# Agent attention and gated FFN: attention arithmetic moved to VectorE, POOL kept for transfers

## The chip, the cores and the metric

The kernel runs on one core of one Trainium2 chip. The metric is the device time of one launch in microseconds (us), lower is better. The times shown are the median of several runs, with the lowest and the highest.

## The reference

Four batches of 12480 tokens with 128 channels, and 49 agents per batch. `agent_v` is the attention of the agents over keys and values; each query then attends to the agents; the result goes through a feed-forward net with 2048 hidden units.

```
def sm(a, b):
    s = scale * (a @ b.transpose(0, 2, 1))
    s = s - s.max(-1, keepdims=True)
    e = np.exp(s)
    return e / (e.sum(-1, keepdims=True) + 1e-09)
agent_v = sm(agents, k) @ v
x = sm(q, agents) @ agent_v          # 4 x 12480 x 128
h = x @ w_in                         # 128 -> 2048
g = h * (1.0 / (1.0 + np.exp(-1.702 * h)))
out = g @ w_out                      # 2048 -> 128
```

All inputs are f32 (the weights arrive as 64-bit floats and are converted on the chip). Queries, keys and agents are scaled by 8, so the softmax is steep and the scores must be exact.

## The kernel before, in words

**Tiling.** A group is 960 tokens (`GT`, two halves of `CH` = 480). A batch has 13 groups (`NG`), and the hidden layer 16 slices of 128 (`NF`). One *step* is one slice of one group, so a batch has 208 steps and the kernel 832. In a step TensorE does `up` (L393: four products of 480 columns into two PSUM banks `ph`, of the pair `sa`, `sb` with the high and the low part of the folded weights `wh`, `wl`), ScalarE the gelu into `g`, and, five steps later (`LAG`), TensorE does `down` (L421: six products of 480 columns into `po`). To keep f32 accuracy with float32r products, `g` is split into a rounded part `gh` (L406) and the rest `gl` = `g` - `gh` (L416, always on VectorE). The rounding is done by a DMA issued from POOL's queue for the slices in `HI_ON_DMA`, by ScalarE for those in `HI_ON_ACT`, and by VectorE otherwise. For a slice rounded by DMA the `gl` subtraction is put two steps later (L671). `g` and `gl` have five tiles each, `gh` six.

**Attention.** It is woven into the steps. `agent_v` of the next batch is folded with `w_in` into `wh`, `wl` (L317, L331), so the feed-forward net takes softmax weights of 49 agents as its input. For that the next batch's 13 key blocks of 960 are loaded, split into three bf16 parts (`split`, L166: four pieces of 484 elements, POOL), multiplied with the agents (`scores`, L180: 32 products into two banks of `ps_m`, each reduced by VectorE at L197), the maximum taken (L240 to L261), and then, per block, shifted (L274, POOL), exponentiated (ScalarE), split into a high and a low part `e_pair` (L282: ScalarE, then POOL) and multiplied with the value block `v_pair`, also split (L288, L291, VectorE); the sums are added up in `acc` (L310). The queries of the next group go through the same `split` and `scores`, a softmax (L352 to L374) and four transposes (`query_pairs`, L377).

**Order.** From step 16 on, the order on TensorE, ScalarE, VectorE and POOL is the order of the program text (`manual_schedule`, L684); each engine's queue is worked off in that order. `put(t, fn)` hangs a job on step t. Within a step come `up`, the jobs, the rounding and `gl`, then `down` of the slice five steps back. `pe_step` (L587) moves a TensorE job to the next step that has none; steps 4 (`Q_AT`) and 13 (`P_AT`) of each group are reserved for query scores and transposes. Key blocks follow at five-step intervals from step 4 of the batch (from step 16 in the first), value blocks at steps 3 and 12 of the groups after that. So a batch has a stage with key blocks, about its first four groups, and a stage with the maximum, the value blocks and the weights; the last batch has neither.

**Buffers around the change.** `ps_m` has two banks for scores, transposes, value sums and weights. `rest` (the parts of a split) and the working tiles have two tiles, the loads `kt`, `vt` together three, `qt` two. `e_pair` and `v_pair` are single. SP issues the loads and the stores.

Of the kernel before, what the change touches and what calls it, by code (L numbers as in the profile page):

```python
# [40 lines left out]
def kernel(  # L41
# [44 lines left out]
    e_pair = const.tile([P, KB, P], F32R, name="e_pair")  # L86
    nc.gpsimd.memset(e_pair.bitcast(F32), 0.0)
# [78 lines left out]
    def split(t):  # L166
        r = work.tile([P, GT + PAD], F32, name="rest", tag="rest")
        nc.gpsimd.memset(t[:, GT:], 0.0)
        n = (GT + PAD) // 2

        def piece(i):
            s = slice(i % 2 * n, (i % 2 + 1) * n)
            if i < 2:
                nc.gpsimd.tensor_sub(out=r[:, s], in0=t[:, s], in1=halves(t)[0][:, s])  # L174
            else:
                nc.gpsimd.tensor_sub(out=halves(r)[1][:, s], in0=r[:, s], in1=halves(r)[0][:, s])  # L176

        return (halves(t)[0], halves(r)[0], halves(r)[1]), piece

    def scores(b, parts, out):  # L180
        x0, x1, x2 = parts
        a = ag_part[:, b].rearrange("p i a -> p (i a)")
        mm = nc.tensor.matmul
        for c in range(2):
            ps = ps_m.tile([P, 512], F32, name="ps_m")
            for j in range(KB // 2):
                t0 = (c * KB // 2 + j) * TB
                t = slice(t0, t0 + P)
                o = ps[:, j * 2 * A : (j + 1) * 2 * A]
                mm(out=o, lhsT=x0[:, t], rhs=a[:, 0 : 2 * A], start=True, stop=False)  # L190
                mm(out=o[:, A:], lhsT=x0[:, t], rhs=a[:, 2 * A :], start=False, stop=False)
                mm(out=o, lhsT=x1[:, t], rhs=a[:, 0 : 2 * A], start=False, stop=False)  # L192
                mm(out=o[:, 0:A], lhsT=x2[:, t], rhs=a[:, 0:A], start=False, stop=True)
            s = ps[:TB, : KB * A].rearrange("p (j i a) -> p j i a", i=2, a=A)
            o = out[:, c * KB // 2 : (c + 1) * KB // 2, :]
            if RED:
                nc.vector.tensor_reduce(out=o, in_=s.rearrange("p j i a -> p j a i"), axis=AX.X, op=ALU.add)  # L197
            else:
                nc.scalar.copy(out=o, in_=s[:, :, 0, :])
                nc.vector.tensor_add(out=o, in0=s[:, :, 1, :], in1=o)  # L200
# [94 lines left out]
    def key_matmuls(g, ps, first, last):  # L295
        for j in range(KB):
            nc.tensor.matmul(  # L297
                out=ps[:, : 2 * C + 2],
                lhsT=e_pair[:TB, j, :],
# [17 lines left out]
    def weights_sums(acc, w):  # L317
        ps = ps_m.tile([P, 512], F32, name="ps_m")
        zc = work.tile([P, P], F32, name="zc", bufs=1)
        nc.vector.tensor_copy(out=zc, in_=acc[:, 2 * C : 2 * C + 1].broadcast_to([P, P]))  # L320
        nc.tensor.matmul(out=ps[:, 0:P], lhsT=acc[:, 0:C], rhs=sel, start=True, stop=False)
        nc.tensor.matmul(out=ps[:, 0:P], lhsT=acc[:, C : 2 * C], rhs=sel, start=False, stop=True)
        nc.tensor.matmul(out=ps[:, P : 2 * P], lhsT=zc, rhs=sel, start=True, stop=True)
# [23 lines left out]
    def query_scores(n, b, parts):  # L347
        sd = e_sb[n % 2][:TB, :, 0:A]
        scores(b, parts, sd)
# [66 lines left out]
    def low(g, gh):  # L416
        gl = gpool.tile([P, 2, CH], F32R, name="gl", bufs=LAG)
# [62 lines left out]
    def do_key_scores(b, g):  # L480
        key_scores(b, g, k_parts.pop((b, g)))
# [99 lines left out]
    pe_steps = {n * NF + f for n in range(B * NG) for f in (Q_AT, P_AT)}  # L581
# [16 lines left out]
    for b in range(B - 1):  # L598
        s0 = b * per_batch
        for k in range(NKG):  # L600
            t = pe_step(s0 + (NF if b == 0 else K_AT) + 5 * k)
            put(t - 13 if b else max(t - 13, 0), lambda b=b, k=k: do_key_load(b + 1, k))
            for i in range(4):
                put(max(t - 5 + i, s0), lambda b=b, k=k, i=i: do_key_split(b + 1, k, i))
# [121 lines left out]
```

## Time and profile before

| | |
|---|---|
| time, median of 3 runs | 2235.41 us (2225.12 to 2239.26) |
| profiled execution | 2236.78 us, span 2235.0 us |
| TensorE (PE) busy | 2108.1 us, 94% of the span |
| VectorE (DVE) busy | 1771.2 us, 79% |
| ScalarE (ACT) busy | 1579.3 us, 71% |
| GpSimd (POOL) busy | 737.7 us, 33% |
| mean granted TensorE clock | 0.979 |
| start of the first step, end of the last group | 73 us, 2224.2 us |

A row of the groups reads: line, engine, operation, output<-inputs with their shapes, count, then busy us and the mean ns of one, then the engine's idle time just before them and what ended most of it. A row of the waits reads: who waited, for whom, us in total, how often, the longest. A row of the stages reads: the stretch, its length, and the busy us of each engine with its instruction count, then granted clock, share of the DMA engines and GB/s. A row of the timeline reads: start, us, engine, line, operation, and in brackets the idle time before it and its releaser.

### The profile page before, as it was taken

What the parts mean: (1) busy time and instruction counts of PE and PEld (TensorE: products, weight loads), DVE (VectorE), ACT (ScalarE), POOL (GpSimd) and SP (SyncE); (2) the same over time, 40 slices, a digit from 0 to 9 for tenths busy, and PEclk for the clock granted to TensorE, in tenths of its full rate; (3) what the DMA queues carried; (4) which work ended last, traced back from release to release, by engine and by line L of the source; (5) the groups of instructions that cost most, each with busy time, mean ns of one, the idle gap of its engine ahead of it and who ended that gap; (6) DMA issues with size and microseconds to landing.
All of it is one profiled execution on the core that took longest, in us unless ns stands there. A gap on an engine that the chain in (4) does not pass through costs nothing.

```text
span 2235.0 us, 32467 instructions
## 1 busy us (share of the span) xinstructions
PE 2108.1 (94%) x12232; PEld 1794.0 (80%) x12232; DVE 1771.2 (79%) x1882; ACT 1579.3 (71%) x2563; POOL 737.7 (33%) x773
## 2 busy tenths in 40 slices
PE   8899998999999999999999999989999999999999
PEld 7688877888777788778778788778877888888887
DVE  6988888778778888888877887887886768776765
ACT  3566776677676678677667667767776887778886
POOL 3355624222135544322214664222221313121310
PEclk9999999999999999999999999999999999999999
DMA  9423412232223232232223233223222221212221
GB/s 263 142 89 107 133 63 80 92 112 80 80 96 99 89 103 93 80 106 98 81 79 106 89 114 108 66 90 114 85 71 71 71 98 63 98 63 87 73 80 62
DMA packets 79297, 210.87 MB, mean 94 GB/s; under 512 B 7580, under 2 KB 33500, under 8 KB 79140
## 3 DMA queue, kind: packets, MB, share of 16 engines
q1 hardware_dynamic: 49188, 106.55, 16.2%
q0 software_dynamic: 29952, 102.25, 13.0%
q8 instruction: 96, 1.57, 0.3%
q14 instruction: 61, 0.50, 0.1%
HBM read 80.97 MB, written 25.56 MB: 48 GB/s over the span
## 4 chain that ended last, share of the span: by engine, by line
PE 69%; DVE 18%; issue 8%; DMA 3%; ACT 1%; POOL 1%; DVEq 0%; ACTq 0%; SPq 0%; POOLq 0%
PE po L429 38%; PE ph L398 12%; PE ph L400 12%; DVE gl L418 11%; DMA gh<-g 2%; DVE gh L413 2%; PE ps_m L190 1%; PE ps_m L213 1%; PE ps_m L192 1%; DVE sb L389 1%; ACT g L403 1%; DVE sa L388 1%; PE ps_m L381 1%; PE ps_m L297 1%; DVE acc L314 1%
## 5 line engine op out<-in xcount | busy, mean ns | idle before, releaser
L418 DVE TENSOR_TENSOR gl<-g,gh 128x960 fp32r<-128x960 f32 x832 | 1131.7, 1385 | 393.1 <-DMA gh<-g 181.7
L403 ACT ACTIVATE g<-ph 128x480 f32<-128x480 f32 x1664 | 857.0, 573 | 424.3 <-PE ph L400 376.1
L429 PE MATMUL po<-gh,wo_h 128*128 128x480 f32 x1664 | 525.8, 397 | 0.2 <-ACT gh L411 0.2
L429 PE MATMUL po<-gl,wo_h 128*128 128x480 f32 x1664 | 503.7, 384 | 11.1 <-DVE gl L418 11.1
L429 PE MATMUL po<-gh,wo_l 128*128 128x480 f32 x1664 | 506.7, 386 | 0.0
L409 POOL DMA_DIRECT2D gh<-g x208 | 115.1, 553 | 1074.7 <-DVE gl L418 714.3
L411 ACT CAST gh<-g 128x960 fp32r<-128x960 f32 x416 | 415.1, 998 | 12.2
L429 PEld LDWEIGHTS po<-gl,wo_h 128*128 128x128 f32 x1664 | 317.2, 191 | 62.8 <-DVE gl L418 12.8
L429 PEld LDWEIGHTS po<-gh,wo_l 128*128 128x128 f32 x1664 | 317.3, 191 | 50.6
L429 PEld LDWEIGHTS po<-gh,wo_h 128*128 128x128 f32 x1664 | 303.2, 191 | 52.6 <-ACT o L440 8.4
L398 PE MATMUL ph<-sb,wh 128*128 128x480 f32 x832 | 320.7, 385 | 0.6 <-DVE sb L389 0.4
L398 PE MATMUL ph<-sa,wh 128*128 128x480 f32 x832 | 320.3, 385 | 0.7 <-ACT g L403 0.7
L400 PE MATMUL ph<-sa,wl 128*128 128x480 f32 x832 | 318.8, 383 | 0.0
L400 PE MATMUL ph<-sb,wl 128*128 128x480 f32 x832 | 316.8, 381 | 0.0
L176 POOL TENSOR_TENSOR rest<-rest 128x484 bf16<-128x484 f32 x182 | 271.1, 1507 | 0.4
L398 PEld LDWEIGHTS ph<-sb,wh 128*128 128x128 f32 x832 | 158.5, 190 | 34.4 <-ACT g L403 5.3
L398 PEld LDWEIGHTS ph<-sa,wh 128*128 128x128 f32 x832 | 159.3, 191 | 30.3 <-ACT g L403 1.4
L400 PEld LDWEIGHTS ph<-sb,wl 128*128 128x128 f32 x832 | 157.4, 189 | 25.7 <-issue 0.2
L400 PEld LDWEIGHTS ph<-sa,wl 128*128 128x128 f32 x832 | 157.7, 190 | 24.9 <-issue 0.2
L413 DVE CAST gh<-g 128x960 fp32r<-128x960 f32 x208 | 164.6, 792 | 2.1 <-ACT g L403 0.3
L174 POOL TENSOR_TENSOR rest<-qt 128x484 f32<-128x484 f32 x104 | 135.8, 1323 | 76.0 <-issue 21.7
L440 ACT COPY o<-po 128x480 f32<-128x480 f32 x104 | 53.2, 564 | 138.2 <-PE po L429 138.2
(103 smaller groups left out, 2055.9 us busy)
## 6 DMA issues: line engine op xcount, KB each, us to landing
gh<-g POOLq DMA_DIRECT2D x208, 480.0 KB, 2.9
kt<-kT SPq DMA_DIRECT2D x52, 480.0 KB, 3.6
qt<-qT SPq DMA_DIRECT2D x52, 480.0 KB, 3.4
vt<-v SPq DMA_DIRECT2D x52, 480.0 KB, 4.2
outT<-o SPq DMA_DIRECT2D x104, 240.0 KB, 2.6
words<-w_in SPq DMA_DIRECT2D x4, 512.0 KB, 11.9
words<-w_out SPq DMA_DIRECT2D x4, 512.0 KB, 8.6
ag_sb<-agT SPq DMA_DIRECT2D x1, 98.0 KB, 2.0
```

The source lines that it names most:

```text
L174: nc.gpsimd.tensor_sub(out=r[:, s], in0=t[:, s], in1=halves(t)[0][:, s])
L176: nc.gpsimd.tensor_sub(out=halves(r)[1][:, s], in0=r[:, s], in1=halves(r)[0][:, s])
L190: mm(out=o, lhsT=x0[:, t], rhs=a[:, 0 : 2 * A], start=True, stop=False)
L398: nc.tensor.matmul(out=ph[c][:, :CH], lhsT=wh[:, s], rhs=pairs[c], start=True, stop=False)
L400: nc.tensor.matmul(out=ph[c][:, :CH], lhsT=wl[:, s], rhs=pairs[c], start=False, stop=True)
L403: nc.scalar.activation(out=g[:, c, :], in_=ph[c][:, :CH], func=AF.Gelu_apprx_sigmoid)
L409: nc.gpsimd.dma_start(out=gh, in_=g)
L411: nc.scalar.copy(out=gh, in_=g)
L413: nc.vector.tensor_copy(out=gh, in_=g)
L418: nc.vector.tensor_sub(out=gl, in0=g, in1=gh.bitcast(F32))
L429: nc.tensor.matmul(out=po[c][:, :CH], lhsT=lhsT[:, f, :], rhs=rhs[:, c, :], start=(f == 0 and first), stop=(f == NF - 1 and last),)
L440: nc.scalar.copy(out=o, in_=po[c][:, :CH])
```

## The change

POOL's arithmetic inside the steps goes to VectorE: the four pieces of each split, now cut so that the first two belong to the first half of the tokens, the key shifts, and the low half of `e_pair`; the high half of `e_pair` goes there from ScalarE. (In the start, ahead of the steps, twelve shifts stay on POOL.) Six slices of 16 instead of four are rounded by DMA, two instead of four by VectorE, eight by ScalarE as before, and the `gl` of a DMA slice is put three steps after its product instead of two. Scores are computed in two pieces of one bank in two steps: steps 4 and 5 for queries, t and the next free step for keys; `e_pair` is doubled, `gl` has four tiles instead of five. Query exponentials move from step 7 to 8, sums and softmax with them, splits from 14 to 15; value blocks from steps 3 and 12 to 1 and 11; the first batch's key blocks start at step 10 instead of 16. The next weights are spaced: the copy `zc` two steps after the last value product, its products two or more after that, the first weight part three or more later. The diff, without the places that only carry the new argument through:

```diff
-E_AT = 7
+E_AT = 8
 P_AT = 13
-S_AT = 14
+S_AT = 15
 K_AT = 4
-V_AT = 3
-V2_AT = 12
+V_AT = 1
+V2_AT = 11
...
-HI_ON_DMA = (7, 8, 9, 11)
-HI_ON_ACT = (0, 2, 5, 6, 10, 12, 14, 15)
+HI_ON_DMA = (1, 3, 5, 10, 11, 14)
+HI_ON_ACT = (0, 2, 4, 6, 7, 12, 13, 15)
...
     def split(t):
         r = work.tile([P, GT + PAD], F32, name="rest", tag="rest")
         nc.gpsimd.memset(t[:, GT:], 0.0)
-        n = (GT + PAD) // 2
         def piece(i):
-            s = slice(i % 2 * n, (i % 2 + 1) * n)
-            if i < 2:
-                nc.gpsimd.tensor_sub(out=r[:, s], in0=t[:, s], in1=halves(t)[0][:, s])
+            s = slice(0, CH + PAD) if i < 2 else slice(CH + PAD, GT + PAD)
+            if i % 2 == 0:
+                nc.vector.tensor_sub(out=r[:, s], in0=t[:, s], in1=halves(t)[0][:, s])
             else:
-                nc.gpsimd.tensor_sub(out=halves(r)[1][:, s], in0=r[:, s], in1=halves(r)[0][:, s])
+                nc.vector.tensor_sub(out=halves(r)[1][:, s], in0=r[:, s], in1=halves(r)[0][:, s])
...
-    def scores(b, parts, out):
+    def scores(b, parts, out, c):
...
-        for c in range(2):
-            ps = ps_m.tile([P, 512], F32, name="ps_m")
+        ps = ps_m.tile([P, 512], F32, name="ps_m")
...
     def key_pair(g):
         sc = score[:TB, g * KB : (g + 1) * KB, :]
-        ep = e_pair
-        nc.scalar.copy(out=ep[:TB, :, 0:A], in_=sc)
-        nc.gpsimd.tensor_sub(out=ep[:TB, :, H : H + A], in0=sc, in1=ep[:TB, :, 0:A].bitcast(F32))
+        ep = e_pair[g % 2]
+        nc.vector.tensor_copy(out=ep[:TB, :, 0:A], in_=sc)
+        nc.vector.tensor_sub(out=ep[:TB, :, H : H + A], in0=sc, in1=ep[:TB, :, 0:A].bitcast(F32))
...
-        gl = gpool.tile([P, 2, CH], F32R, name="gl", bufs=LAG)
+        gl = gpool.tile([P, 2, CH], F32R, name="gl", bufs=LAG - 1)
...
-    pe_steps = {n * NF + f for n in range(B * NG) for f in (Q_AT, P_AT)}
+    pe_steps = {n * NF + f for n in range(B * NG) for f in (Q_AT, Q_AT + 1, P_AT)}
...
-            t = pe_step(s0 + (NF if b == 0 else K_AT) + 5 * k)
+            t = pe_step(s0 + (10 if b == 0 else K_AT) + 5 * k)
+            t1 = pe_step(t + 1)
...
-            put(t, lambda b=b, k=k: do_key_scores(b + 1, k))
-            put(t + 1, lambda k=k: key_part_max(k))
+            put(t, lambda b=b, k=k: do_key_scores(b + 1, k, 0))
+            put(t1, lambda b=b, k=k: do_key_scores(b + 1, k, 1))
+            put(t1 + 1, lambda k=k: key_part_max(k))
...
-            put(min(shift + 3 * k, slot - 1), lambda k=k: key_shift(k, nc.gpsimd.tensor_tensor))
+            put(min(shift + 3 * k, slot - 1), lambda k=k: key_shift(k, nc.vector.tensor_tensor))
             put(t - 16, lambda b=b, k=k: do_value_load(b + 1, k))
-            put(t - 3, lambda k=k: key_pair(k))
-            put(t - 4, lambda b=b, k=k: value_hi(k, vts[b + 1, k]))
-            put(t - 4, lambda b=b, k=k: value_lo(k, vts.pop((b + 1, k))))
+            put(t - 3, lambda b=b, k=k: value_hi(k, vts[b + 1, k]))
+            put(t - 3, lambda b=b, k=k: value_lo(k, vts.pop((b + 1, k))))
+            put(slot + 1, lambda k=k: key_pair(k))
...
-        put(pe_step(last + 2), lambda b=b, w=w: weights_sums(accs.pop(b + 1), w))
-        t = last + 3
+        put(t + 2, lambda b=b, w=w: weights_0(accs.pop(b + 1), w))
+        t = pe_step(t + 4)
+        put(t, lambda w=w: weights_1(w))
+        t = t + 2
...
-        put(s0 + Q_AT, lambda n=n: do_query_scores(n + 1))
-        put(s0 + Q_AT + 1, lambda n=n: do_query_load(n + 2))
-        put(s0 + Q_AT + 1, lambda n=n: do_query_shift(n + 1))
+        for c in range(2):
+            put(s0 + Q_AT + c, lambda n=n, c=c: do_query_scores(n + 1, c))
+        put(s0 + Q_AT + 2, lambda n=n: do_query_load(n + 2))
+        put(s0 + Q_AT + 2, lambda n=n: do_query_shift(n + 1))
...
-                at.setdefault(t + 2, []).insert(0, lambda t=t: live.update({t: (gh, low(g, gh))}))
+                at.setdefault(t + 3, []).insert(0, lambda t=t: live.update({t: (gh, low(g, gh))}))
```

`weights_0` holds the copy `zc` and `weights_1` the rest of the former `weights_sums`.

More of the change, by code (lines that the diff above doesn't have):

```diff
@@ L84 @@
         )
-    e_pair = const.tile([P, KB, P], F32R, name="e_pair")
-    nc.gpsimd.memset(e_pair.bitcast(F32), 0.0)
+    e_pair = []
+    for i in range(2):
+        t = const.tile([P, KB, P], F32R, name=f"e_pair{i}")
+        nc.gpsimd.memset(t.bitcast(F32), 0.0)
+        e_pair.append(t)
     v_pair = const.tile([P, KB, 2 * C + 2], F32R, name="v_pair")
@@ L183, in scores @@
         mm = nc.tensor.matmul
-        for c in range(2):
-            ps = ps_m.tile([P, 512], F32, name="ps_m")
[L186 to L200, printed above, removed]
+        ps = ps_m.tile([P, 512], F32, name="ps_m")
+        for j in range(KB // 2):
+            t0 = (c * KB // 2 + j) * TB
+            t = slice(t0, t0 + P)
+            o = ps[:, j * 2 * A : (j + 1) * 2 * A]
+            mm(out=o, lhsT=x0[:, t], rhs=a[:, 0 : 2 * A], start=True, stop=False)
+            mm(out=o[:, A:], lhsT=x0[:, t], rhs=a[:, 2 * A :], start=False, stop=False)
+            mm(out=o, lhsT=x1[:, t], rhs=a[:, 0 : 2 * A], start=False, stop=False)
+            mm(out=o[:, 0:A], lhsT=x2[:, t], rhs=a[:, 0:A], start=False, stop=True)
+        s = ps[:TB, : KB * A].rearrange("p (j i a) -> p j a i", i=2, a=A)
+        o = out[:, c * KB // 2 : (c + 1) * KB // 2, :]
+        nc.vector.tensor_reduce(out=o, in_=s, axis=AX.X, op=ALU.add)
     def key_load(b, g):
@@ L228, in first_key_scores, with key_scores @@
         )
-    def key_scores(b, g, parts):
-        s = score[:TB, g * KB : (g + 1) * KB, :]
-        scores(b, parts, s)
+    def key_scores(b, g, parts, c):
+        scores(b, parts, score[:TB, g * KB : (g + 1) * KB, :], c)
     def key_part_max(g):
@@ L298, in key_matmuls @@
                 out=ps[:, : 2 * C + 2],
-                lhsT=e_pair[:TB, j, :],
+                lhsT=e_pair[g % 2][:TB, j, :],
                 rhs=v_pair[:TB, j, :],
@@ L314, in key_sum, with weights_0, weights_1 @@
             nc.vector.tensor_add(out=acc, in0=ps[:, : 2 * C + 1], in1=acc)
-    def weights_sums(acc, w):
-        ps = ps_m.tile([P, 512], F32, name="ps_m")
+    def weights_0(acc, w):
         zc = work.tile([P, P], F32, name="zc", bufs=1)
         nc.vector.tensor_copy(out=zc, in_=acc[:, 2 * C : 2 * C + 1].broadcast_to([P, P]))
-        nc.tensor.matmul(out=ps[:, 0:P], lhsT=acc[:, 0:C], rhs=sel, start=True, stop=False)
-        nc.tensor.matmul(out=ps[:, 0:P], lhsT=acc[:, C : 2 * C], rhs=sel, start=False, stop=True)
-        nc.tensor.matmul(out=ps[:, P : 2 * P], lhsT=zc, rhs=sel, start=True, stop=True)
+        w["acc"], w["zc"] = acc, zc
+    def weights_1(w):
+        ps = ps_m.tile([P, 512], F32, name="ps_m")
+        nc.tensor.matmul(out=ps[:, 0:P], lhsT=w["acc"][:, 0:C], rhs=sel, start=True, stop=False)
+        nc.tensor.matmul(out=ps[:, 0:P], lhsT=w["acc"][:, C : 2 * C], rhs=sel, start=False, stop=True)
+        nc.tensor.matmul(out=ps[:, P : 2 * P], lhsT=w["zc"], rhs=sel, start=True, stop=True)
         rz = work.tile([P, P], F32, name="rz", bufs=1)
@@ L345, in query_load, with query_scores @@
         return t
[L347 removed]
+    def query_scores(n, b, parts, c):
         sd = e_sb[n % 2][:TB, :, 0:A]
[L349 removed]
+        scores(b, parts, sd, c)
         return sd
```

28 lines of the change are left out of this document (14 added, 14 removed).

## The prediction

> **What bounds the kernel now.** I read the page first, then the engines' busy time by stage, the list of waits, and the timeline of one group where a wait ends.
>
> ```profile
> PE 2108.1 (94%) x12232; PEld 1794.0 (80%) x12232; DVE 1771.2 (79%) x1882; ACT 1579.3 (71%) x2563; POOL 737.7 (33%) x773
> ```
>
> TensorE is the long engine. A step is ten 480-column products, a group 16 steps, a batch 13 groups. The next rows cut the span at group borders (us, then busy time of PE, PEld, DVE, ACT, POOL, granted clock, DMA). Each of the first three batches has a key stage (rows 1, 3, 5: five, four and four groups, in which the next batch's 13 key blocks are scored) and a value stage (rows 2, 4, 6: eight, nine and nine groups, with 13 value blocks, the maximum and the next weights). Row 7 is the last batch, row 8 four of its groups.
>
> ```profile
> core 0: us, PE busy (x) PEld busy (x) DVE busy (x) ACT busy (x) POOL busy (x), PEclk, DMA share, GB/s
> 73.00:290.80 217.80, 203.23 (x1373) 170.18 (x1372) 194.66 (x216) 149.74 (x240) 113.11 (x109) 0.97 0.33 103
> 290.80:640.70 349.90, 323.15 (x1689) 273.89 (x1689) 277.18 (x280) 245.29 (x400) 97.08 (x104) 0.96 0.27 87
> 640.70:814.70 174.00, 164.57 (x1170) 140.45 (x1169) 144.07 (x153) 117.36 (x188) 90.93 (x95) 0.98 0.33 103
> 814.70:1190.80 376.10, 356.01 (x1917) 301.91 (x1916) 302.64 (x314) 274.51 (x448) 106.76 (x111) 0.98 0.28 90
> 1190.80:1360.90 170.10, 162.44 (x1169) 138.11 (x1169) 145.08 (x155) 118.19 (x189) 104.07 (x99) 1.00 0.33 105
> 1360.90:1743.40 382.50, 357.51 (x1918) 303.29 (x1918) 306.25 (x316) 274.68 (x448) 100.09 (x108) 0.98 0.26 84
> 1743.40:2224.20 480.80, 477.57 (x2514) 408.09 (x2513) 352.49 (x370) 378.71 (x607) 99.68 (x107) 1.00 0.22 78
> 1743.40:1890.10 146.70, 146.70 (x786) 125.64 (x784) 109.57 (x117) 117.67 (x189) 36.97 (x36) 1.00 0.24 81
> 900.00:942.00 42.00, 37.26 (x197) 31.90 (x196) 33.34 (x35) 28.16 (x47) 11.86 (x14) 0.92 0.29 93
> 942.00:984.00 42.00, 39.77 (x217) 33.95 (x216) 34.73 (x37) 30.93 (x51) 10.71 (x12) 1.00 0.30 95
> ```
>
> Row 8 gives TensorE's floor: 146.7/4 = 36.7 us a group, clock 1.00, never idle. The other batches pay more, partly for extra products, the rest for waits:
>
> ```profile
> PE ps_m L190 <- DVE acc L314: 46.8, 18, 5.1
> PE ps_m L190 <- DVE sb L389: 12.4, 6, 2.8
> PE po L429 <- DVE gl L418: 11.1, 4, 4.2
> PE ps_m L381 <- DVE score L197: 9.2, 3, 4.5
> PE ps_m L321 <- DVE acc L314: 7.3, 3, 2.5
> PE ps_m L381 <- DVE p_pad L370: 7.2, 4, 2.9
> PE ps_m L323 <- DVE zc L320: 6.9, 3, 2.7
> PE ps_m L250 <- DVE mx L242: 6.1, 4, 2.7
> PE po L555 <- DMA vt<-v: 3.3, 5, 0.7
> ```
>
> All but the last are VectorE handing on a PSUM bank or a small tile late. After the longest the clock falls (0.92 in the row from 900, 1.00 in the next), so a wait costs more than its length. The timeline shows the commonest:
>
> ```profile
> 987.03 1.13 PE L297 MATMUL ps_m<-v_pair,e_pair 120*128 120x258 f32 x8
> 988.18 2.23 DVE L418 TENSOR_TENSOR gl<-g,gh 128x960 fp32r<-128x960 f32 x2
> 991.08 1.16 DVE L418 TENSOR_TENSOR gl<-g,gh 128x960 fp32r<-128x960 f32 x1
> 992.27 0.43 DVE L314 TENSOR_TENSOR acc<-ps_m,acc 128x257 f32<-128x257 f32 x1
> 992.76 0.22 PE L190 MATMUL ps_m<-ag_part,qt 128*128 128x98 bf16 x1 [1.83 <-DVE acc L314]
> 993.34 0.68 PE L429 MATMUL po<-gh,wo_h 128*128 128x480 f32 x2
> ```
>
> The value product fills a bank one step ahead of the query scores. Those need two banks at once, and the second is free only after the `acc` addition, which stands on VectorE behind three `gl` subtractions. VectorE is late because its instructions are long:
>
> ```profile
> L418 DVE TENSOR_TENSOR gl<-g,gh 128x960 fp32r<-128x960 f32 x832 | 1131.7, 1385 | 393.1 <-DMA gh<-g 181.7 <-ACT gh L411 121.0 <-PE ph L400 60.9
> L176 POOL TENSOR_TENSOR rest<-rest 128x484 bf16<-128x484 f32 x182 | 271.1, 1507 | 0.4
> L174 POOL TENSOR_TENSOR rest<-qt 128x484 f32<-128x484 f32 x104 | 135.8, 1323 | 76.0 <-issue 21.7 <-DVE m L134 19.6 <-DMA qt<-qT 18.5
> L413 DVE CAST gh<-g 128x960 fp32r<-128x960 f32 x208 | 164.6, 792 | 2.1 <-ACT g L403 0.3
> L276 DVE TENSOR_TENSOR score<-score,max_b 120x392 f32<-120x392 f32 x1 | 0.6, 566 | 0.0
> L409 POOL DMA_DIRECT2D gh<-g x208 | 115.1, 553 | 1074.7 <-DVE gl L418 714.3 <-ACT g L403 351.0 <-issue 5.2
> 982.91 3.79 DVE L418 TENSOR_TENSOR gl<-g,gh 128x960 fp32r<-128x960 f32 x2
> 983.78 3.78 POOL L176 TENSOR_TENSOR rest<-rest 128x484 bf16<-128x484 f32 x2
> ```
>
> A `gl` takes 1.16 us alone (991.08), and two overlap by 0.09 us (2.23 at 988.18). Beside POOL subtractions two take 3.79 us, and POOL's two 3.78: they block each other. The mean of 1385 against 1160 is 0.225 x 832 = 187 us of VectorE time lost.
>
> **The change part by part.**
>
> *Splits move to VectorE.* (52 + 39) x 4 = 364 pieces of 484 elements. Subtractions of 392 and 960 elements take 0.566 and 1.16 us, a slope of 1.05 ns an element, so 484 take 0.66 us, 0.57 after the overlap: 207 us. POOL's own 1.5 us is the upper bound, as no row shows VectorE writing every second bf16; below 0.57 nothing speaks. I take 0.57, interpolated on the engine that will do it. Shifts and both halves of the key pairs add 39 x (0.48 + 0.28 + 0.48) = 48 us; the 0.28 is a 392-element copy scaled from the cast row. ScalarE and POOL lose that work, off the path.
>
> *Contention goes*: -187 us on `gl`. Casts go from four a group at 0.79 to two at 0.66: 165 to 69 us, -96. The other contended lines I put at -25, an estimate. VectorE's sum: 1771 + 207 + 48 - 187 - 96 - 25 = about 1718 us. The engine is not relieved; its load moves into the key stages.
>
> *Key stage of batch 1* (row 3): VectorE 144.1 + (13 + 4) x 4 x 0.57 = +38.8, `gl` 64 x 0.225 = -14.4, casts 16 x 0.79 - 8 x 0.66 = -7.4, others -3: 158 us. TensorE's floor is 4 x 36.7 + 13 x 2 banks x 0.58 (992.76 to 993.34) = 162 us. So VectorE stands at 97% of TensorE. It sat idle 174 - 144 = 30 us there. Of that the DMA waits, 181.7/208 x 16 = 14 us, should go, because `gl` of a slice rounded by DMA now comes three steps after its product, a 2.2 us step more, and a transfer lands quickly:
>
> ```profile
> DMA to landing us min/median/max: 2.8/2.9/6.1
> ```
>
> New idle comes in. `rest` still has two tiles, and scores now end one to three steps later. By the step table, at 12 places the first piece of a key split stands in VectorE's order one (9 times) or two (3 times) steps ahead of the score product that frees its tile. Behind it wait `gl` and the reduction that frees a score bank; at the three, the next key piece on TensorE then waits about 1.2 us. `gl` has four tiles instead of five: slices 9 and 15 wait for products two steps later, and slice 14 comes out just when TensorE wants it. So 10 to 24 us of idle: 158 + 10 = 168 us, against 174. Bounds: 162 (TensorE alone) and 182 (24 us). Row 5 likewise 168; row 1, where the weight conversions already fill VectorE (195 of 218), 214.
>
> *Value stages.* The score pieces take one bank each in steps 4 and 5, and value products move to steps 1 and 11, so `acc` has three steps to clear: the 46.8 us and its clock losses go. Weights: `zc` now precedes its product by two steps, 7.3 + 6.9 us go. What takes its place: VectorE's steps 8 and 9 hold two `gl` more, a value pair (1.9 us), two key pairs (1.5, into an `e_pair` that is now double) and two casts, about 8 us in two steps; by that queue `e_pair` and `p_pad` are ready within 0.2 us of TensorE's use. I allow 0.5 us a group, bounds 0 and the old 2 us. Nine groups: 9 x 36.7 + 13 x 1.1 (987.03) + 8 weight products of 0.65 = 350 us, + 5 = 355. Eight: 313 + 4 = 317.
>
> ```profile
> L337 PE MATMUL ps_m<-w_in_sb,avT 128*128 128x512 f32 x32 | 17.9, 654 | 3.0 <-DVE avT L328 2.9
> ```
>
> *Six slices on DMA.* 312 issues of 0.553 us are 173 us on POOL, otherwise nearly idle; its queue holds no arithmetic any more, so an issue follows its gelu at once.
>
> The Trainium skill, "SBUF — State Buffer", section "Who interferes with whom", speaks against this part: a transfer issued from POOL's queue can be held up while VectorE copies in its two-port mode (3.1 us instead of 0.62 in the example of the section "A bandwidth-pool intuition that's wrong"). By that rule, an estimate from the page: 2.5 us later each would exceed the 2.2 us of added room by 0.3 us, some 25 us of the key stages, and the end would be near 2164. The row of landings (median 2.9, minimum 2.8 beside 208 VectorE casts) does not show it.
>
> *Queues and the start.* Loads on SP come one step later for queries and hold their tiles up to three steps longer for keys; they land in a few us and have five steps or more. The first query's four pieces (2.3 us) now stand on VectorE ahead of the maximum; the first value products wait for loads anyhow (the `vt` row), so I cost them at 0, at most 2.4 us. Keys of batch 1 start six steps earlier, which only shifts load.
>
> *Sum.* 214 + 317 + 168 + 355 + 168 + 355 + 478 = 2055 us, against 217.8 + 349.9 + 174.0 + 376.1 + 170.1 + 382.5 + 480.8 = 2151.2. The saving is 96 us; in the last batch 3 us for one wait. The profiled execution's span is 2235.0 (its own time 2236.8, the median of the runs 2235.4), so 2235 - 96 = **2139 us**.
>
> **Rivals.**
> - *Every wait goes*: stages at the floors, 199 (5 x 36.7 + 15) + 313 + 162 + 350 + 162 + 350 + 477 = 2013, saving 138: 2097 us. For it: row 8 runs so, with VectorE at 75%. Against: 97% in the key stage.
> - *VectorE keeps its idle time in the key stages* because the `rest` waits replace the DMA waits: 158 + 24 = 182 us twice and 14 more in row 1: 2139 + 42 = 2181.
> - *Value waits only move* to `e_pair` or `p_pad`: the 46.8 us stay, 2186.
> - *The pieces cost on VectorE what they cost on POOL*, 1.5 us, because of the two-byte reads and writes at every second place: 0.84 us more x 208 pieces in the three key stages = 175, less 3 x 16 us of idle that takes it up: 2139 + 127 = 2266. From 1.35 us a piece, (96 + 48)/208 above mine, the kernel is slower than before. For it: POOL's two rows. Against it: those hold contention, and VectorE's own rows follow the element count alone.
> - *The clock or POOL's transfers behave otherwise and nothing is won*: about 2235.
>
> **How the numbers follow.** Forecast 0.50 (own range 2110 to 2165), all waits gone 0.17, key-stage idle 0.15, value waits 0.10, slow pieces 0.05, nothing won 0.03. The range takes in the second to fourth case: 2097 to 2196. A measurement of this kernel can tell about 1%, 22 us, from no change. Faster by more than that needs under 2213: the first four cases, less a little for two of them together, 0.88. Within 1%: 0.07. Slower: 0.05.
>
> **What would show it.** Right: pieces on VectorE near 0.66 us, `gl` mean near 1160, VectorE busy near 1718 us, POOL below 220; no wait of L190 on `acc`, granted clock above 0.985; value stages near 355, key stages near 168. Wrong: pieces above 1.3 us; key stages above 182; new waits of TensorE on `e_pair`, `p_pad` or `gl` of 40 us or more; VectorE still waiting over 100 us for `gh` transfers.

## The result, and the profile after

The changed kernel takes 2118.11 us (median of 4 runs, 2117.56 to 2119.75); the kernel before took 2233.55 us in the same session (2225.12 to 2239.26). The ratio is 0.9487, with a 95% interval of 0.9455 to 0.9519: 115 us or 5.1% faster. The forecast was 2139 with a range of 2097 to 2196. The profiled execution took 2118.66 us, with a span of 2116.9 and a mean granted clock of 0.994.

The first line of the page of the kernel after, busy time by engine:

```profile
PE 2085.7 (99%) x12232; PEld 1769.1 (84%) x12232; DVE 1741.0 (82%) x2259; ACT 1563.2 (74%) x2524; POOL 195.9 (9%) x436
```

TensorE went from 94% to 99% of a shorter span. VectorE's busy time even fell by 30 us (from 1771.2) although it took over POOL's 364 pieces, 39 key shifts and both halves of 39 key pairs; the time that it no longer loses to POOL, and two casts a group, paid for them. The stage rows of the kernel after, cut at the same group borders as those of before (stretch, length, busy us of PE, PEld, DVE, ACT, POOL, granted clock, DMA share, GB/s):

```profile
75.16:282.26 207.10, 202.93 (x1375) 167.62 (x1373) 192.30 (x273) 148.34 (x240) 19.11 (x47) 0.98 0.41 131
282.26:596.35 314.09, 313.07 (x1687) 265.42 (x1686) 260.86 (x335) 240.94 (x388) 26.85 (x57) 1.00 0.37 121
596.35:760.42 164.07, 163.21 (x1169) 136.89 (x1168) 152.81 (x211) 117.55 (x189) 14.41 (x40) 1.00 0.41 133
760.42:1113.26 352.84, 352.06 (x1918) 297.92 (x1916) 292.66 (x375) 270.24 (x435) 30.02 (x64) 1.00 0.37 121
1113.26:1277.22 163.96, 163.11 (x1169) 137.15 (x1168) 152.70 (x211) 117.58 (x189) 14.88 (x40) 1.00 0.41 133
1277.22:1629.20 351.98, 351.58 (x1918) 297.79 (x1916) 292.60 (x375) 270.31 (x435) 29.89 (x63) 1.00 0.36 117
1629.20:2106.10 476.90, 476.70 (x2515) 407.83 (x2514) 341.33 (x390) 377.76 (x607) 42.42 (x89) 1.00 0.31 106
```

From the second row on, TensorE is busy for all but a microsecond or so of each stage. Against before, the value stages (rows 2, 4, 6) gained 36, 23 and 31 us, the key stages (rows 1, 3, 5) 11, 10 and 6, the last batch 4.

The groups of the kernel after that answer to the ones shown of before, shapes kept apart (count, then busy us and mean ns of one, then idle time before and what ended it):

```profile
L416 DVE TENSOR_TENSOR gl<-g,gh 128x960 fp32r<-128x960 f32 x832 | 951.1, 1156 | 249.6 <-ACT gh L409 200.0 <-PE po L427 35.5 <-DMA gh<-g 0.5
L407 POOL DMA_DIRECT2D gh<-g x312 | 167.8, 538 | 1836.7 <-ACT g L401 1163.5 <-DVE e_sb L196 175.5 <-DVE gl L416 164.5
L411 DVE CAST gh<-g 128x960 fp32r<-128x960 f32 x104 | 68.2, 656 | 13.0 <-ACT g L401 13.0
L177 DVE TENSOR_TENSOR rest<-rest 128x488 bf16<-128x488 f32 x91 | 65.9, 725 | 0.0
L177 DVE TENSOR_TENSOR rest<-rest 128x480 bf16<-128x480 f32 x91 | 65.4, 718 | 0.6
L175 DVE TENSOR_TENSOR rest<-qt 128x488 f32<-128x488 f32 x52 | 34.3, 659 | 0.0
```

The `gl` mean is 1156 ns, where 1385 stood: no `gl` is held up by POOL any more. A piece that took POOL 1.3 to 1.5 us takes VectorE 0.66 or 0.72. The longest waits of TensorE inside the steps, in the list of waits of the kernel after, are these four:

```profile
PE po L427 <- DVE gl L416: 2.2, 1, 2.2
PE ps_m L190 <- DVE e_sb L196: 1.9, 3, 0.6
PE ps_m L292 <- DVE e_pair L281: 1.8, 6, 0.5
PE ps_m L379 <- DVE p_pad L368: 0.9, 4, 0.3
```

The wait of L190 for `acc` (46.8 us) is gone, the others of the old list are, inside the steps, gone or under 3 us, and nothing long took their place. (What is left of the wait for `mx`, one of 3.9 us, lies in the start.) On VectorE, in the same list, the wait for DMA of 181.7 us has shrunk to the 0.5 us in the row above, and the wait for a `rest` tile that the forecast reckoned with is there:

```profile
DVE gl L416 <- ACT gh L409: 200.0, 214, 4.2
DVE rest L175 <- PE ps_m L193: 18.7, 9, 3.7
```

### The profile page after: what moved, and what is told of

It is laid out like the page before. It is cut to its first block, busy times and chain, and to the rows that moved or that the text cites. A ratio compares the mean times of both kernels' runs of the same rounds, so it can differ in the third digit from the quotient of the medians.

```text
span 2116.9 us, 32655 instructions
## 1 busy us (share of the span) xinstructions
PE 2085.7 (99%) x12232; PEld 1769.1 (84%) x12232; DVE 1741.0 (82%) x2259; ACT 1563.2 (74%) x2524; POOL 195.9 (9%) x436
## 3 DMA queue, kind: packets, MB, share of 16 engines
q1 hardware_dynamic: 49188, 106.55, 17.7%
## 4 chain that ended last, share of the span: by engine, by line
PE 92%; DVE 6%; DMA 1%; issue 1%; ACT 0%; ACTq 0%; SPq 0%; DVEq 0%; POOLq 0%
PE po L427 50%; PE ph L396 16%; PE ph L398 16%; PE ps_m L292 2%; DVE gl L416 2%; PE ps_m L190 2%; PE ps_m L192 1%; PE ps_m L209 1%; PE ps_m L379 1%; PE ps_m L191 1%; PE ps_m L193 1%; PE ps_m L335 1%; DMA words<-w_out 0%; DVE rest L175 0%; DVE v_pair L288 0%
## 5 line engine op out<-in xcount | busy, mean ns | idle before, releaser
L416 DVE TENSOR_TENSOR gl<-g,gh 128x960 fp32r<-128x960 f32 x832 | 951.1, 1156 | 249.6 <-ACT gh L409 200.0
L427 PE MATMUL po<-gl,wo_h 128*128 128x480 f32 x1664 | 498.1, 381 | 2.2 <-DVE gl L416 2.2
L407 POOL DMA_DIRECT2D gh<-g x312 | 167.8, 538 | 1836.7 <-ACT g L401 1163.5
L427 PEld LDWEIGHTS po<-gh,wo_h 128*128 128x128 f32 x1664 | 292.7, 189 | 39.9 <-issue 5.7
L177 DVE TENSOR_TENSOR rest<-rest 128x488 bf16<-128x488 f32 (+1 forms) x182 | 130.2, 721 | 0.6
L192 PE MATMUL ps_m<-ag_part,rest 128*128 128x98 bf16 x728 | 114.9, 205 | 0.0
L193 PE MATMUL ps_m<-ag_part,rest 128*128 128x49 bf16 x728 | 111.4, 187 | 0.0
L196 DVE TENSOR_REDUCE e_sb<-ps_m 120x196 f32<-120x392 f32 x104 | 58.9, 566 | 37.0 <-PE ps_m L193 36.9
```

The source lines that it names most:

```text
L177: nc.vector.tensor_sub(out=halves(r)[1][:, s], in0=r[:, s], in1=halves(r)[0][:, s])
L196: nc.vector.tensor_reduce(out=o, in_=s, axis=AX.X, op=ALU.add)
L407: nc.gpsimd.dma_start(out=gh, in_=g)
L416: nc.vector.tensor_sub(out=gl, in0=g, in1=gh.bitcast(F32))
L427: nc.tensor.matmul(out=po[c][:, :CH], lhsT=lhsT[:, f, :], rhs=rhs[:, c, :], start=(f == 0 and first), stop=(f == NF - 1 and last),)
```

## The experiments

Three questions: which part of the change brings the gain; how near VectorE now stands to the bound; and what the smaller parts (six DMA slices, the third step for `gl`, one-bank scores, the start) are worth. On the first there were two theories. *Schedule*: what pays is where the bank users stand, above all the value blocks three steps ahead of the query scores, so that `acc` clears in time; VectorE's speed matters little. *Contention*: what pays is that POOL's arithmetic no longer blocks VectorE; with `gl` back at 1.16 us the old order would do.

The stage columns below are read from each kernel's stage rows like those above: row 3 (key stage of batch 1, with VectorE's busy time) and row 4 (its value stage). The ratios are to the kernel before, run in the same session; between sessions that kernel's median moved from 2225 to 2234 us, so experiments are compared by ratio and by stage.

| kernel | median us | ratio, 95% interval | key stage (VectorE) | value stage |
|---|---|---|---|---|
| before | 2233.55 | 1 | 174.0 (144.1) | 376.2 |
| changed | 2118.11 | 0.9487 [0.9455, 0.9519] | 164.1 (152.8) | 352.8 |
| e1 changed, arithmetic on POOL | 2171.39 | 0.9716 [0.9679, 0.9753] | 170.0 (143.8) | 364.9 |
| e2 before, value blocks spaced | 2182.62 | 0.9771 [0.9738, 0.9803] | 173.5 (146.7) | 363.5 |
| e3 before, arithmetic on VectorE | 2187.04 | 0.9792 [0.9758, 0.9826] | 171.2 (156.7) | 367.5 |
| e10 e2 and e3 together | 2155.80 | 0.9684 [0.9656, 0.9713] | 171.4 (156.7) | 357.6 |
| e9 changed, half the pieces twice | 2164.83 | 0.9703 [0.9658, 0.9748] | 176.8 (172.1) | 353.3 |
| e5 changed, every piece twice | 2238.96 | 1.0036 [1.0017, 1.0055] | 200.2 (195.4) | 354.4 |
| e6 changed, idle work on POOL | 2255.81 | 1.0108 [1.0069, 1.0148] | 201.9 (196.2) | 363.6 |
| e4 changed, DMA slices two steps later | 2119.82 | 0.9490 [0.9460, 0.9520] | 163.2 (152.8) | 354.0 |
| e8 changed, the four old DMA slices | 2112.24 | 0.9463 [0.9426, 0.9499] | 164.7 (157.0) | 350.3 |
| e12 changed, scores in one step | 2113.41 | 0.9493 [0.9467, 0.9520] | 163.3 (153.1) | 352.2 |
| e11 e8, first query split on POOL | 2112.17 | 0.9489 [0.9463, 0.9515] | 164.7 (157.1) | 350.4 |
| e13 changed, exponentials at step 7 | 2139.45 | 0.9569 [0.9537, 0.9601] | 163.4 (152.0) | 358.7 |

### e1: the new schedule with the arithmetic back on POOL

```diff
-                nc.vector.tensor_sub(out=r[:, s], in0=t[:, s], in1=halves(t)[0][:, s])
+                nc.gpsimd.tensor_sub(out=r[:, s], in0=t[:, s], in1=halves(t)[0][:, s])
...
-                nc.vector.tensor_sub(out=halves(r)[1][:, s], in0=r[:, s], in1=halves(r)[0][:, s])
+                nc.gpsimd.tensor_sub(out=halves(r)[1][:, s], in0=r[:, s], in1=halves(r)[0][:, s])
```

The key shifts and the low half of `e_pair` go back to POOL in the same way.

> The changed kernel (median 2118 us) with the split pieces, the key shifts and the low half of the key pairs back on POOL; its order of steps, its one-bank score pieces and its six DMA slices stay. Theory S (spacing: the gain in the value stages comes from when the banks are asked for): the waits of L190 on the acc addition stay below 5 us, value stages stay near 353 us, only the key stages go back towards 170 to 174 us; time 2130 to 2150. Theory C (contention: VectorE was late because POOL's subtractions stretch gl): gl mean back near 1380 ns, waits of TensorE on VectorE over 60 us, time 2190 to 2235. In both, POOL's arithmetic now also delays its DMA issues, some us more.

2171.39 us, a little over half of the gain. The `gl` row and the waits of TensorE in this kernel:

```profile
L416 DVE TENSOR_TENSOR gl<-g,gh 128x960 fp32r<-128x960 f32 x832 | 1142.9, 1392 | 312.2 <-ACT gh L409 228.9 <-PE po L427 42.8 <-DMA gh<-g 17.2
```

```profile
PE ps_m L292 <- DVE v_pair L288: 19.4, 16, 1.4
PE ps_m L379 <- DVE p_pad L368: 11.1, 4, 4.0
PE ps_m L292 <- POOL e_pair L281: 10.5, 21, 0.9
PE po L427 <- DVE gl L416: 8.5, 12, 2.3
```

The contention is back in full (1392 ns), and still no wait for `acc` is left. But the operands of the value products are now late. So the schedule removes the old wait by itself, and the arithmetic on VectorE is what keeps `v_pair`, `e_pair` and `p_pad` from taking its place. The time lies between the ranges of the two theories: neither holds alone.

### e2: two constants in the kernel before

```diff
-V_AT = 3
-V2_AT = 12
+V_AT = 1
+V2_AT = 11
```

> The kernel before (2234 us) with one thing of the change: value blocks at steps 1 and 11 instead of 3 and 12, so that the acc addition has three steps before the query scores ask for its bank. Theory S: the 46.8 us of L190 on acc go, with some 10 to 20 us of half clock behind them: 2165 to 2185. Theory C: VectorE stays late, the wait moves to another bank or to gl: 2215 to 2235.

2182.62 us: the schedule's figure. The `acc` wait is gone, and a value stage falls from 376.2 to 363.5 us. The key stage stays (173.5). TensorE now waits longer for `zc` of the weights than before (6.9 us there):

```profile
PE ps_m L323 <- DVE zc L320: 15.3, 3, 5.3
```

### e3: the arithmetic on VectorE in the kernel before

The edit of e1 the other way, with the old order, the old four DMA slices and the high half of `e_pair` on ScalarE.

> The kernel before with one thing of the change: POOL's arithmetic inside the steps (split pieces, key shifts, low half of the key pairs) on VectorE, everything else as before. gl mean near 1160 ns in both theories. Theory C: most of the gain is there, 2130 to 2165. Theory S: three gl still stand ahead of the acc addition and two banks are still asked for in one step, so the value stages keep most of their waits, and the key stages carry the pieces with four VectorE casts a group and the DMA waits: 2195 to 2240.

2187.04 us. The contention theory's number is refuted; the schedule theory's was too pessimistic. `gl` falls to 1154 ns, as it should, and half of the old wait remains:

```profile
PE ps_m L190 <- DVE acc L314: 23.5, 18, 2.1
```

### e10: both in the kernel before

The edits of e2 and e3 together.

> The kernel before with the value blocks at steps 1 and 11 and with the splits, key shifts and low halves of the pairs on VectorE; scores in one step, four slices by DMA, one e_pair, the weights unspaced. Theory A (the two parts add up, since they remove different waits: the spacing those on acc, the move the length of gl): 2233.5 - 51 - 46.5 = 2136, between 2126 and 2146, so that all else in the change is worth 10 to 28 us against the changed kernel's 2118. Theory B (they remove the same delay of VectorE's queue, and the rest of the change supplies what is missing): 2155 to 2175. Under A the bank waits left are those of L190 on sb and of the weights (zc, acc), 20 to 30 us in all; under B more than 45 us of them.

2155.80 us is B's time; but of the waits for banks, those that A named (`sb`, `zc`) come to 22 us, within its 20 to 30:

```profile
PE ps_m L190 <- DVE sb L389: 14.7, 7, 3.3
PE ps_m L250 <- DVE mx L242: 12.3, 4, 3.9
PE ps_m L323 <- DVE zc L320: 7.2, 3, 2.4
```

The stages show why each is half right. In the value stage of batch 1 the two parts add up nearly: 376.2 less 12.7 (e2) less 8.7 (e3) would be 354.8; it is 357.6. Over the three value stages they do not: e2 saves 53 us there, e3 46, both together 79, where the whole change saves 90. So some 20 us are a delay that either part removes, as B says. In the key stages almost nothing is won: the whole change saves 27 us in the three of them, the two parts together under 2. In that of batch 1 VectorE is idle for 171.4 - 156.7 = 15 us, and over the whole run it waits for its own inputs, for DMA above all:

```profile
DVE gl L418 <- DMA gh<-g: 126.2, 59, 4.6
DVE e_pair L286 <- ACT e_pair L285: 70.4, 21, 3.5
```

So the last 2% of the 5.1% (0.9684 to 0.9487) come from the rest of the edit: 25 of the 35 us between the sums of the stages lie in the key stages. How its parts divide them is open. e4, e8 and e12 below each take one part back (the third step, the six DMA slices, the scores in two steps), and the key stages of batches 1 and 2 stay at 163.2 to 164.7 us: none of the three is needed alone. Two of them together were not run, nor the later maximum, the pair on VectorE and the earlier keys of batch 1 by themselves.

### e9 and e5: VectorE's load doubled in part

Pieces 0 and 2 (e9), or all four (e5), are written twice, with the same values.

```diff
-                nc.vector.tensor_sub(out=r[:, s], in0=t[:, s], in1=halves(t)[0][:, s])
+                for _ in range(2):
+                    nc.vector.tensor_sub(out=r[:, s], in0=t[:, s], in1=halves(t)[0][:, s])
```

> The changed kernel with two of the four pieces (the f32 ones) computed twice: VectorE's key stage load 153 + 34 x 0.57 = 172 us, 8 us above the changed kernel's stage of 164 us. Theory A (load plus 11 us idle): 183 us a key stage, 2160 to 2180. Theory B (load alone): 172 us, 2136 to 2150. Theory C (room): 2117 to 2125.

> The changed kernel with each of the four split pieces computed twice on VectorE (the same result written again): a piece then costs about 1.25 us of VectorE time, as near as this comes to the rival of slow pieces, which was priced at 1.5 us and said to decide from 1.35 us. VectorE's key stage load goes from 153 us (changed kernel, 164 us stage) to 153 + 68 x 0.57 = 192 us. Theory A (load plus the 11 us of idle time that the changed kernel shows there): 203 us a key stage, first stage some 33 us longer, value stages unchanged, 2220 to 2235. Theory B (load alone): 192 us and 25 longer, 2192 to 2210. Theory C (VectorE has room): under 2150.

2164.83 and 2238.96 us. Their rows of the key stage of batch 1, e9 and then e5:

```profile
613.28:790.12 176.84, 165.75 (x1170) 137.49 (x1168) 172.14 (x243) 117.91 (x189) 14.48 (x40) 0.99 0.39 124
```

```profile
638.83:839.04 200.21, 173.38 (x1170) 142.26 (x1168) 195.42 (x276) 118.45 (x189) 14.95 (x40) 0.96 0.34 110
```

The stage is VectorE's busy time plus about 5 us in both (172.1 + 4.7, 195.4 + 4.8; in batch 2 plus 6.0 and 5.4), while the value stages hardly move (353.3, 354.4). That lies between theories A (plus 11) and B (plus nothing); the time of e9 is in A's range, that of e5 is 4 us above it, since its first stage grew by 41 us where 33 were expected. By the same sum the changed kernel's VectorE would need 152.8 + 5 = 158 us, and TensorE's 163 stands above it: 5 to 6 us a key stage were free, and the rest of e9's 19 us came out as time (176.8 against 164.1). The clock falls too as TensorE waits more (1.00, 0.99, 0.96). The waits in e5 are those of work behind a full queue:

```profile
PE ps_m L381 <- DVE p_pad L370: 33.4, 12, 4.8
PE ps_m L192 <- DVE e_sb L198: 23.0, 9, 3.6
PE po L429 <- DVE gl L418: 20.3, 18, 2.5
```

### e6: idle arithmetic on POOL beside each piece

The changed kernel, and beside each piece a POOL subtraction of 484 elements that reads a constant and writes a tile of its own, which nothing reads.

```diff
+            nc.gpsimd.tensor_sub(out=idle_o, in0=idle_i, in1=idle_i)
```

> The changed kernel with a subtraction of 484 elements on POOL beside each VectorE piece; nothing reads its result. POOL's load and the contention come back, but nothing depends on POOL's arithmetic and VectorE keeps its pieces. Theory C (contention alone has a price): gl mean 1300 to 1400 ns, VectorE's key stage load near 170 us, value groups near 41 us as with the splits on POOL (2171): 2160 to 2200. Rival (POOL's arithmetic cost time because its results came late): 2118 to 2135.

2255.81 us, slower than the kernel before, and far above what was expected. VectorE issues the same instructions on the same data; they only take longer:

```profile
L420 DVE TENSOR_TENSOR gl<-g,gh 128x960 fp32r<-128x960 f32 x832 | 1088.2, 1327 | 184.0 <-ACT gh L413 145.2 <-PE po L431 25.7 <-DMA gh<-g 0.5
L181 DVE TENSOR_TENSOR rest<-rest 128x488 bf16<-128x488 f32 x91 | 91.6, 1006 | 0.0
L179 DVE TENSOR_TENSOR rest<-qt 128x488 f32<-128x488 f32 x52 | 60.8, 1168 | 0.0
```

Nothing reads POOL's results here, and `gl` still waits only 0.5 us for transfers, so it is not that POOL issues them late: the contention is shown by itself. It is dear because it falls into the key stages, where VectorE has 5 to 6 us to spare: VectorE's busy time in that of batch 1 rises from 152.8 to 196.2, and the stage from 164.1 to 201.9. The three key stages take 104 of the 138 us.

### e4: `gl` of a DMA slice two steps after its product, as before

```diff
-                at.setdefault(t + 3, []).insert(0, lambda t=t: live.update({t: (gh, low(g, gh))}))
+                at.setdefault(t + 2, []).insert(0, lambda t=t: live.update({t: (gh, low(g, gh))}))
```

> The changed kernel with the gl of a DMA slice two steps after its product instead of three. VectorE's waits for gh transfers come back: 312 of them at about 0.9 us each by the 181.7 us over 208 before, some 200 us or more of VectorE idle time. Theory as predicted (key stages are set by VectorE's load plus its idle time, the rest is hidden): key stages 164 to 174, value stages within 3 us, time 2135 to 2155. Rival (VectorE has room everywhere now): 2117 to 2123.

2119.82 us (2118.73 to 2121.28), within 2 us: the rival's case. VectorE's waits in this kernel:

```profile
DVE gl L416 <- PE po L427: 136.8, 173, 2.2
DVE gl L416 <- DMA gh<-g: 17.7, 24, 2.3
```

The transfers are in time even at two steps; what the `gl` waits for instead is one of its four tiles. The third step was worth under 2 us here. The 181.7 us of before were thus no matter of that step alone. Nor of the slices alone: e8, with the four old slices (7, 8, 9 and 11, close together) and three steps, waits 30.6 us for transfers, while e10, with these slices and two steps, waits 126.2.

### e8: the four old DMA slices in the changed kernel

```diff
-HI_ON_DMA = (1, 3, 5, 10, 11, 14)
-HI_ON_ACT = (0, 2, 4, 6, 7, 12, 13, 15)
+HI_ON_DMA = (7, 8, 9, 11)
+HI_ON_ACT = (0, 2, 5, 6, 10, 12, 14, 15)
```

> The changed kernel with the four DMA slices and eight ScalarE slices of the kernel before (four casts a group on VectorE instead of two), gl of a DMA slice still three steps later. VectorE gains 104 casts, some 70 to 80 us in all, 6 us a key stage. If the six slices matter because VectorE is near its bound in the key stages: 2130 to 2150. If VectorE has room: 2117 to 2125. Slices 7, 8, 9 land together behind the exponentials, which could add waits of their own: some us more in either case.

2112.24 us (2111.80 to 2112.72): below both cases, 6 us under the changed kernel, and with e11 the fastest median. The intervals of the two ratios overlap, since the kernel before scatters by more than that; the stage rows show the difference (seven stages sum to 2023.6 us against 2030.5). VectorE carries 39 us more, yet the value stages fall by 2.7, 2.5 and 2.1 us; the key stages of batches 1 and 2 rise by 0.6 and 0.7. Where those microseconds go shows in step 11 of a value group, which holds a value product. On TensorE, first the changed kernel, then e8:

```profile
941.83 0.37 PE L396 MATMUL ph<-sa,wh 128*128 128x480 f32 x1
943.45 1.20 PE L292 MATMUL ps_m<-v_pair,e_pair 120*128 120x258 f32 x8 [0.39 <-DVE e_pair L281]
945.80 0.38 PE L396 MATMUL ph<-sa,wh 128*128 128x480 f32 x1
```

```profile
938.93 0.38 PE L396 MATMUL ph<-sa,wh 128*128 128x480 f32 x1
940.01 1.14 PE L292 MATMUL ps_m<-v_pair,e_pair 120*128 120x258 f32 x8
942.29 0.38 PE L396 MATMUL ph<-sa,wh 128*128 128x480 f32 x1
```

The step takes 945.80 - 941.83 = 3.97 us there and 3.36 here. This group is the slowest of its batch; over eight such groups it is 3.67 and 3.36. The changed kernel's product waits for `e_pair`, for the most part ahead of its weight loads: these stand idle 21 times, 10.1 us in all, and not at all in e8. Why the pairs are late shows on ScalarE and VectorE in the same group, first of the changed kernel, then of e8:

```profile
938.91 0.84 ACT L275 ACTIVATE score<-score 120x784 f32<-120x784 f32 x1
936.04 2.34 DVE L416 TENSOR_TENSOR gl<-g,gh 128x960 fp32r<-128x960 f32 x2 [1.02 <-ACT gh L409]
938.29 0.69 DVE L284 CAST v_pair<-vt 120x1024 fp32r<-120x1024 f32 x1
939.02 1.23 DVE L288 TENSOR_TENSOR v_pair<-vt,v_pair 120x1024 fp32r<-120x1024 f32 x1
940.16 0.66 DVE L411 CAST gh<-g 128x960 fp32r<-128x960 f32 x1
941.27 1.16 DVE L416 TENSOR_TENSOR gl<-g,gh 128x960 fp32r<-128x960 f32 x1 [0.46 <-DVE gh L411]
942.35 0.36 DVE L280 CAST e_pair<-score 120x392 fp32r<-120x392 f32 x1
```

```profile
936.00 0.85 ACT L275 ACTIVATE score<-score 120x784 f32<-120x784 f32 x1
936.88 0.37 DVE L280 CAST e_pair<-score 120x392 fp32r<-120x392 f32 x1 [1.66 <-ACT score L275]
```

The exponentials end 2.08 us before step 11 begins in both (939.75 before 941.83, 936.85 before 938.93), so they are not late. In e8 the pairs follow them at once. In the changed kernel VectorE is behind: it first works off two `gl`, one of them slice 7 after ScalarE's cast, the value pair, and the cast and the `gl` of slice 8, and the pairs begin 2.6 us after the exponentials. In e8 a DMA rounds slices 7, 8 and 9, and their `gl` come three steps later, behind the pairs. This is read from these rows; the place of slices 7 and 8 was not changed by itself.

### e13: the exponentials a step earlier

```diff
-E_AT = 8
+E_AT = 7
```

> The changed kernel with all exponentials at step 7 instead of 8 (E_AT), so that the key pairs are made in step 8 and are ready a step before the value product of step 11; the six DMA slices stay. In the changed kernel a value group costs 39.17 us, of which step 11 takes 3.67 us, 0.52 more than step 1 with the same product; with the four slices of before 3.36. Theory A (step 11 waits for e_pair, which the ScalarE cast of slice 7 ahead of the exponentials delays, and this is what the six slices cost): step 11 falls to 3.2 to 3.4 us, value groups to 38.7 to 38.9, the time by 5 to 10 us to 2108 to 2114. Theory B (the six slices cost by their transfers, not by the order): step 11 stays above 3.55 us and the time within 2116 to 2121. Against A: query scores end in step 5, so their shift in step 6 leaves the exponentials less room; if ScalarE then waits over 1 us a group for it, the time rises to 2125 or more.

2139.45 us, 21 us slower. Step 11 fell to 3.15 us, a little further than A expected, so `e_pair` was what it waited for. This does not show that the cast of slice 7 delayed the exponentials: the edit also moves the pairs a step ahead, before the cast and the `gl` of slice 8 on VectorE, and the rows under e8 put the delay there. Steps 9 and 10 together rose from 4.37 to 5.47 us, and each group of the last batch from 36.7 to 37.0. ScalarE's cast of slice 7 now stands behind the exponentials, with the second table load ahead of the gelus of the next slices (4.8 us pass without a gelu, where 3.9 did), and TensorE waits for those:

```profile
PE ph L396 <- ACT g L401: 11.6, 23, 0.6
```

A's time was missed by 25 us, and the danger that the expectation named (the shift too late) is not what happened.

### e12: both score pieces in one step

```diff
-            put(t1, lambda b=b, k=k: do_key_scores(b + 1, k, 1))
+            put(t, lambda b=b, k=k: do_key_scores(b + 1, k, 1))
...
-            put(s0 + Q_AT + c, lambda n=n, c=c: do_query_scores(n + 1, c))
+            put(s0 + Q_AT, lambda n=n, c=c: do_query_scores(n + 1, c))
```

> The changed kernel with both pieces of a score product again in one step (query scores both in step 4, key scores both in step t), all else where it was. Theory A (the pieces in two steps do little once value blocks stand three steps ahead): 2113 to 2123, TensorE's waits for banks before L190 under 6 us, and VectorE's waits for rest tiles fall from 18.7 to under 10 us since scores end earlier. Theory B (one bank at a time is what keeps TensorE from waiting for the reduction before): 2128 to 2145, with 10 us or more of waits at L190 for sb, the score reduction or other banks.

0.9493, no difference to the changed kernel by ratio, 5 us by the sum of the stages (2025.1); the key stage is 0.7 us shorter, TensorE's waits at L190 for a bank are 5.0 us in all, and VectorE's for `rest` have left its list. With value blocks three steps ahead, scores in two steps are not needed: theory A.

### e11: the first query's split on POOL again

The kernel of e8; the four pieces of query 0 are issued on POOL, all later ones on VectorE.

> The changed kernel with the four DMA slices and the slices of the kernel before (2112.2 us measured), and the first query's four split pieces on POOL as in the kernel before. Theory A (these pieces ahead of the maximum delay the start by 2.2 us): the first step begins 2 to 2.5 us earlier and the time is 2109 to 2111. Theory B (the start is held by loads and the 2.2 us come from elsewhere, the clock or the order of the weights): first step and time unchanged within 1 us, 2111.5 to 2113.

2112.17 us against 2112.24: B's time, though the first step does begin 1.6 us earlier. The first group takes that back. The row of the first group in e8, then in e11:

```profile
75.48:114.71 39.23, 36.05 (x221) 27.69 (x219) 38.53 (x63) 31.69 (x52) 2.71 (x8) 0.99 0.35 113
```

```profile
73.92:115.75 41.83, 37.51 (x220) 27.91 (x218) 40.55 (x68) 31.66 (x52) 2.71 (x8) 0.97 0.33 106
```

VectorE is busy for all but 0.7 and 1.3 us of it, the weight conversions among its work. That the group ends with that queue, however early it starts, is argued from these rows and not shown.

## Why the prediction was right, point by point

**The mechanism held.** `gl` fell to 1156 ns (1160 forecast), VectorE's busy time to 1741 (1718), POOL's to 196 (below 220), no L190 waits for `acc`, the clock is 0.994 (above 0.985). e2 and e6 show the two causes apart: the place of the value blocks, and POOL's blocking of VectorE. What the forecast did not say is how they depend on each other: each alone brings some 2%, both together 3.2%, and a last 2% needs the rest of the edit as well (e10).

**The 21 us too many.** Forecast and measured stage by stage: 214 and 207.1, 317 and 314.1, 168 and 164.1, 355 and 352.8, 168 and 164.0, 355 and 352.0, 478 and 476.9, together 24 us less than forecast, less 2.2 for the later start. The largest terms are the key stages, 7 + 4 + 4 = 15. There the step "158 + 10 = 168 us" was mis-sized in its first term: VectorE needed 152.8, not 158. The forecast took the time lost to POOL at the mean of the whole span, 1385 ns a `gl` and 792 a cast, while the pieces stand closer in a key stage: there the means before were 1452 and 959. So `gl` gave back 18.6 us (91.2 to 72.5) where 14.4 were put down, and the casts 10.0 (15.3 to 5.3) where 7.4 were. Its idle time, forecast as 10 to 24, was 11. So the stage came out at TensorE's floor, 162 forecast and 163.2 busy, and not at VectorE's sum. The other 9 are the value stages' allowance and the last batch.

**Pieces.** Writing f32 they take 0.655 us, as interpolated (0.66). Writing every second bf16 they take 0.72: 182 x 0.06 = 11 us of the 23 us by which VectorE's sum was low. How the other 12 divide (the 25 us put on other contended lines is one candidate) was not separated.

**The `rest` waits** are there, 9 times and 18.7 us in all, where 12 were read off the step table. They stay on VectorE; TensorE, said to wait 1.2 us at three places, shows no such wait. VectorE has 5 to 6 us to spare in a key stage, by e9. With four tiles instead of five, `gl` waited 35.5 us for a free one, and TensorE for `gl` 2.2.

**DMA slices.** That their waits would go "because" of the third step was half of the cause: with the six slices, two steps bring back only 17.7 us of them, and 1.7 us of time (e4), and with the four old slices, three steps leave 30.6 (e8). Either of the two edits removes most of the 181.7. That six slices would help VectorE was right, and useless: four are 6 us faster (e8), because, by the rows under e8, the new choice puts `gl` of slices 7 and 8 and a cast ahead of the pairs on VectorE. That is the queue "in steps 8 and 9" for which the forecast allowed 0.5 us a group. Step 11 loses that much, 3.67 us against the 3.15 of e13, where the pair is ready; the mechanism was foreseen, but the 0.5 was not worked out, and that it fits so well is luck.

The Trainium skill's rule in "SBUF — State Buffer", section "Who interferes with whom", that transfers from POOL's queue are held up by VectorE's two-port copies, is not seen here: `gl` waited for DMA 0.5 us in all, beside 104 casts on VectorE and 312 transfers, which landed in 2.8 us by the median (2.9 before). Whether these casts are two-port copies no run here shows. The Trainium skill's rule in the same section, that a VectorE instruction with two SBUF inputs contends with a POOL instruction that reads SBUF, agrees with e6 (`gl` from 1156 to 1327 ns) and with e1 (1392).

**The start**, costed at 0 with a bound of 2.4 us, came 2.2 us later (75.16 against 72.96); e11 shows that starting earlier gains nothing. The 0 was right, but the reason given (the first products wait for loads anyhow) was not: in the start TensorE's wait for `vt` did shrink from 3.3 to 0.4 us, but those for `mx` and `acc` grew by 1.2 and 2.5. The first group, in which VectorE is hardly ever idle, gives the lead back; that its queue is the cause is argued, as under e11.

**The rivals.** "Every wait goes" (2097) was missed by 21 us, as far as the forecast on the other side; of these 8 are in row 1 (207.1 against 199), 6 in the value stages, 4 in the key stages and 2 in the start. The idle time in the key stages was there but cost nothing. The value waits did move, to `e_pair`, at 0.5 us a group. For "slow pieces" the turning point was put at 0.69 us more for each piece. In e5 each piece costs VectorE (1966.9 - 1741.0)/364 = 0.62 us more, and the kernel is 0.4% slower than before: the point lies at about 0.6, not far from what was worked out.

## What to carry to other kernels

When a wait is for a PSUM bank, first look at how many steps lie between its last writer and its next user: two constants (e2) brought 2.3% with no work removed. Moving arithmetic off an engine that blocks another pays only as far as the bound stage has room, so sum each engine's work stage by stage and not over the span, with the durations of that stage: here 5 to 6 us of spare VectorE time a key stage decided between a free move and a loss. And choose which slices an engine converts by what stands behind them in its queue, not by its load: the freer VectorE of the six slices lost to the busier one of four, whose queue left the key pairs free.

## What the hardware showed that was not expected

- POOL subtractions that share no data with VectorE raise its time in a key stage from 152.8 to 196.2 us (e6); 364 of them cost 138 us of kernel time.
- Two subtractions of the same length on VectorE differ by 10% with their output: 0.655 us into f32, 0.72 into every second bf16.
- The exponentials cost two table loads of 1.28 us a group on ScalarE, and moving them a step, with what hangs on them, cost 21 us (e13) though ScalarE is busy only 74% of the span.
